# The last transform's second half: whole rows in 4 KB runs read in step 14, and the rows of the last two steps read over them from DRAM buffers of their own

## The chip, the cores and the metric

The kernel runs on one core of one Trainium2 chip. The time is the device time of one execution in microseconds (us). The core has the engines PE (matrix products), DVE, ACT and POOL (elementwise work) and SP, which here only issues DMA copies; ACT and POOL issue some copies too. Sixteen DMA engines move the data of the copies.

## The reference

One layer on 2048 rows of 512 channels in float32. Three of its lines matter here:

```python
h = _layernorm(x, axis=-1) * (1 + ca) + sa
x = x + ga * _A_ref(h, ...)        # long convolution, one filter of 2048 taps per channel
x = x + gb * _B_ref(_layernorm(x) * (1 + cb) + sb, ...)   # shift mixing and an MLP
```

`_A_ref` builds the filter K from the state-space parameters, multiplies the spectra of the padded filter and the padded input, transforms back and keeps the first 2048 rows:

```python
Yf = Uf * Kf[None, :, :, :]
y = irfft2(Yf, s=(1, L2))[:, :, 0, :L]
```

The change lies in this transform back.

## The kernel before, in words

First the kernel builds the filter, normalises the input and stores the first part of its transform in DRAM (`VU`); this takes up to about 225 us, and its long loop runs small pieces of other work from lists called `side`, one list per turn. From 345 us on it only mixes (`_B_ref`). Between lie the sixteen steps (225 to 306 us) and the last transform.

A step is a pair (jh, kc): jh is the half of the 512 channels, kc one of eight groups of four frequencies k1. Step n multiplies the spectra of its group (`spectrum_k` at line 680, `multiply` at 690 and 692), and the step after it runs `back` (702) for it: eight matmuls with `Gm`, two ACT evictions into a tile z of 128 partitions by 4 by 256, and two stores of 256 KB each on POOL's queue into the DRAM buffer `ZT[jh]` (706). z holds for each of 64 output columns j, twice (real and imaginary part n), the group's four frequencies.

The last transform (`inv_half`, line 731) needs for its column block k (four columns j; eight blocks per half of the channels) the rows of all 32 frequencies. So `load_inv` (721) reads a block of 512 KB that gathers from the stores of all eight steps of a half: 128 partitions by 4 by 256, into one of seven buffers of the pool `ldp`, which also holds the `VU` loads. An output group g of `inv_half` needs four blocks: groups 0 and 3 need blocks 3, 7, 0, 4, groups 1 and 2 need 1, 5, 2, 6. Each `inv_half` is 32 matmuls, and DVE adds the result to X2.

The order is written by hand. For half 0: blocks 0, 3, 4, 7 are issued in step 10 on SP, group 0 runs in step 12, group 3 in step 13, blocks 1, 2, 5, 6 are issued in step 13, group 1 runs after step 15 and group 2 behind it. For half 1 nothing is read before the last store: `back` of step 15 stores in two halves on SP's and ACT's queues, then come blocks 3, 7, 0, 4 in halves on both queues, blocks 1, 5, 2, 6 on SP, then a few matmuls that fill the time (`keep`), then group 3's half at 313.63 us and so on with mixing between, group 1 first at 325.52 us.

Each engine works in its own program order. A DMA-issuing instruction waits in that order too, so what SP has to wait for holds back all copies behind it. The framework adds the waits: a load waits for the stores that wrote what it reads (all eight steps of the half), and for the last reader of its buffer.

Of the kernel before, what the change touches and what calls it, by code (L numbers as in the profile page):

```python
# [7 lines left out]
F32 = mybir.dt.float32  # L8
# [19 lines left out]
def shape_constants():  # L28
    f = lambda x: np.ascontiguousarray(x.astype(np.float32))
    k1, k2, q = np.arange(32), np.arange(64), np.arange(32)  # L30
    c2b = lambda c: np.where(c < 32, 31 - c, c)
    th = 2 * np.pi * (k1[None] + .5) * q[:, None] / 64
    W = np.stack([np.cos(th), -np.sin(th)], 1)
    Wt = W.transpose(0, 2, 1)
    FU = np.stack([np.stack([Wt, -Wt[..., ::-1]], 1), np.stack([Wt, Wt[..., ::-1]], 1)])
    FU = np.stack([FU, FU])
    FK = np.zeros((2, 2, 32, 2, 64))
    FK[:, 0, :, 0] = FK[:, 1, :, 1] = W.reshape(32, 64)
    b = c2b(np.arange(64))
    al = 2 * np.pi * b[:, None, None] * ((k1[None, :, None] + .5) / 4096 + k2[None, None, :] / 64)  # L40
    c, s = np.cos(al), np.sin(al)
    T2 = np.stack([np.stack([c, -s], 2), np.stack([s, c], 2)]).reshape(128, 32 * 128)
    be = np.arange(32) + .5
    al = 2 * np.pi * be[:, None, None] * ((k1[None, :, None] + .5) / 4096 + k2[None, None, :] / 64)
    TU = np.stack([np.cos(al), np.sin(al), np.cos(al), -np.sin(al)]).reshape(128, 32 * 64)
    al = 2 * np.pi * be[None, :] * k2[:, None] / 64
    cs = np.stack([np.cos(al), np.sin(al)], 2).reshape(64, 64)
    Gm = np.tile(np.concatenate([cs, cs], 1), (2, 1))
    sg = np.array([1.0, -1.0])[:, None]
    th = 2 * np.pi * (k1[:, None, None, None] + .5) * (sg * be[:, None, None] + 64 * q) / 4096  # L50
    FI = np.stack([np.cos(th), -sg * np.sin(th), -np.sin(th), -sg * np.cos(th)]) * (2 / 4096)
    eye = np.eye(16)
    j = np.arange(32)
    c0 = np.tile((eye[:, :, None] * (j + .5)).reshape(16, 512), (2, 1))
    C0 = np.zeros((2, 2, 32, 2, 512))
    C0[:, 0, :, 0], C0[:, 1, :, 1] = c0, c0
    C0 = C0.reshape(128, 1024)
    e1 = (eye[:, :, None] * j).reshape(16, 512)
    e2 = (eye[:, :, None] * np.ones(32)).reshape(16, 512)
    C1 = np.concatenate([e1, e1, e2, e2] * 2, 0)  # L60
    ex0 = np.concatenate([np.arange(31, -1, -1), np.arange(32, 64)])
    ex1 = np.concatenate([64 * np.arange(8), 512 * np.arange(4)])
    CE = np.concatenate([(eye[:, :, None] * ex0.reshape(2, 32)[:, None, None, :]).transpose(1, 0, 2, 3).reshape(16, -1),
                         np.zeros((16, 64 * NX1))], 1)
    CE = np.tile(CE, (8, 1))
    for u in range(4):
        CE[u * 32:u * 32 + 32, 1024 + u * 16 * NX1:1024 + (u + 1) * 16 * NX1] = \
            np.tile((eye[:, :, None] * ex1).reshape(16, -1), (2, 1))
    PA = np.zeros((2, 4, 16, 2, 2, 4, 2, 16))
    PB = np.zeros((4, 2, 16, 4, 4, 2, 4, 16))  # L70
    for e in range(16):
        for v in range(2):
            for u in range(4):
                for p in range(2):
                    PA[v, u, e, v, p, u, p, e] = 1
        for c in range(8):
            for p in range(4):
                PB[c // 2, c % 2, e, c // 4 * 2 + c % 2, p, 1 - c // 2 % 2, p, e] = 1
    return {k: f(v) for k, v in dict(
        FU=FU.reshape(128, 128), FK=FK.reshape(128, 128), T2=T2, TU=TU, G=Gm,  # L80
        FI=FI.reshape(128, 32 * 64), C0=C0, C1=C1, CE=CE, PA=PA.reshape(128, 512), PB=PB.reshape(128, 2048), ID=np.eye(128)).items()}

# [20 lines left out]
def dram(t, off, ap):  # L103
    return bass.AP(tensor=t.tensor, offset=t.offset + off, ap=ap)


def body(ctx, tc, A):
    nc = tc.nc
    V, S, P, T, Y = nc.vector, nc.scalar, nc.gpsimd, nc.tensor, nc.sync
    pool = lambda name, bufs=1, **k: tc.tile_pool(name=name, bufs=bufs, **k)  # L110
    glob = ctx.enter_context(pool("glob"))
    dpool = ctx.enter_context(pool("dscr", space=DRAM))
# [3 lines left out]

    VU = dpool.tile([2, 64, 64, 256], F32, name="VU")
    ZT = [dpool.tile([128, 32, 256], F32, name=f"ZT{i}") for i in range(2)]
    GD = dpool.tile([4, 128, 20, 128], F32, name="GD")
    WD = {k: dpool.tile(list(A[k].shape), F32, name="D" + k) for k in ("w2", "w3", "w4")}  # L120

# [52 lines left out]
    up = a12.enter_context(pool("up", bufs=2))  # L174
# [15 lines left out]
    C0 = ph.tile([128, 1024], F32R, name="C0")  # L190
# [315 lines left out]
    side = {k: [] for k in range(40)}  # L506
    for k in range(8):
        w, i = ("w3", k) if k < 4 else ("w4", k - 4)
# [26 lines left out]
    def load_tu():  # L535
        TU.append(wml.tile([128, 32, 64], F32, name="wm"))
        Y.dma_start(TU[0], A["TU"].rearrange("p (a b) -> p a b", a=32))

    side[24].append(load_t2)
    side[29].append(load_tu)  # L540
    side[31].append(load_t2)
# [153 lines left out]
    def back(jh, kc):  # L695
        zc = zcs.pop((jh, kc))
        z = s2.tile([128, 4, 256], F32, name="z")
        o = [psa.tile([128, 2, 256], F32, name="pz") for kk in range(2)]
        for n in range(2):
            for kk in range(2):  # L700
                r = slice(kk * 64, kk * 64 + 64)
                T.matmul(o[kk][n * 64:n * 64 + 64], Gm[r, n], zc[n][r], start=True, stop=True, skip_group_check=True)

        def store(q, a, b):
            for n in range(2):
                q.dma_start(dram(ZT[jh], n * 16384 + (kc * 4 + a) * 256, [[32768, 32], [8192, 2], [1, (b - a) * 256]]),
                            z[n * 64:n * 64 + 64, a:b].rearrange("p k d -> p (k d)"))

        last = (jh, kc) == (1, 7)
        for kk in range(2):  # L710
            act(z[:, 2 * kk:2 * kk + 2], o[kk])
            if last:
                store((Y, S)[kk], 2 * kk, 2 * kk + 2)
        if not last:
            store(P, 0, 4)

    def load_inv(jh, k, i=None, q=Y):
        if (jh, k) not in zis:
            zis[jh, k] = block()
        a, n = (0, 4) if i is None else (2 * i, 2)  # L720
        q.dma_start(zis[jh, k][:, a:a + n], dram(ZT[jh], (k * 4 + a) * 32768, [[256, 128], [32768, n], [1, 256]]))

    def load_x(g):
        Y.dma_start(X2[:, g * 4:g * 4 + 4].rearrange("p b d -> p (b d)"), A["x"][g])
# [372 lines left out]
    with tc.manual_schedule():  # L1097
# [11 lines left out]
        for n, st in enumerate(steps):  # L1109
            p = spectrum_k(*st)  # L1110
            multiply(*st, us, p)
            if n == 7:
                v0x.close()
                pw2 = ctx.enter_context(pool("pw2", side="right", reuse_waits="tile"))
                pw1 = ctx.enter_context(pool("pw1", side="right", reuse_waits="tile"))
                W2h, W2l, ldw2 = weights(pw2, WD["w2"], 512, 512, "w2", 4)
                W1h, W1l, ldw1 = weights(pw1, A["w1"], 512, 512, "w1", 4)
            if n > 0:
                back(*steps[n - 1])
            if n == 15:  # L1120
                i1 = inverse_parts(0, 1, psb, "pk2")
            if n < 15:
                us = spectrum_u(*steps[n + 1])
            if n + 3 < 16:
                load_vu(*steps[n + 3])
            if n % 2 == 0 and n < 14:
                flip(steps[n + 2][1])
            if n in (3, 4, 6, 8):
                load_x(n - 3 if n < 5 else n // 2 - 1)
            if n == 9:  # L1130
                Y.dma_start(FI, A["FI"].rearrange("p (a b c) -> p a b c", a=32, b=2))
            if split:
                split()
                split = None
            if n in (8, 9):
                split = ldw1(two, n % 2 * 2, 2)
            if n == 10:
                for k in (0, 3, 4, 7):
                    load_inv(0, k)
            if n == 12:  # L1140
                inverse(0, 0)
                w2s = [ldw2(None, 2 * i, 2) for i in range(2)]
                for b in range(4):
                    half_stat(b, 0)
            if n == 13:
                inverse(0, 3)
                for k in (1, 2, 5, 6):
                    load_inv(0, k)
            if n in (14, 15):
                w2s.pop()()  # L1150
        for f in i1:
            f()
        back(*steps[15])
# [10 lines left out]
            for _ in range(n):  # L1164
                T.matmul(d, W1h[:, 0, :128], W1h[:, 0], start=True, stop=True)

        for k, i in ((3, 1), (0, 0)):
            load_inv(1, k, i, Y)
            load_inv(1, k + 4, i, S)
        for k, i in ((3, 0), (0, 1)):  # L1170
            load_inv(1, k, i)
            load_inv(1, k + 4, i)
        for i in range(2):
            inv_half(0, 2, i, psy, "py")()
        for b in (14, 15, 4, 5, 6, 7):
            half_stat(b, 0)
        for k in (1, 2):
            load_inv(1, k)
            load_inv(1, k + 4)
        keep(6)  # L1180
        inv_half(1, 3, 1, psy, "py")()
        first_stats(7)
# [119 lines left out]
```

## Time and profile before

| | |
|---|---|
| median of three runs | 689.6 us (687.0, 689.6, 690.3) |
| profiled execution | 691.26 us, its span 689.5 us, mean granted clock 0.989 |
| PE busy | 642.6 us, 93% of the span |
| DVE, ACT, POOL busy | 498.0, 331.2, 124.8 us |
| DMA | 86.42 MB, 125 GB/s over the span |
| chain that ended last | PE 70%, DVE 6%, DMA 5%, ACT 3% |

The profile gives, for each stretch of time, each engine's busy time with the number of instructions, the clock granted to PE, the share of time in which the 16 DMA engines were busy, and GB/s. A row of the timeline has start, duration, engine, line, operation, output and inputs; in brackets stands how long the engine had been idle before, and what it waited for. SPq and ACTq are the queues in which SP and ACT issue copies; the duration there is that of issuing. In the DMA views a packet is one run of contiguous bytes.

### The profile page before, as it was taken

To read this page: it belongs to the slowest core of one execution; us is meant where nothing else is said; L and a number is where in the kernel's file an instruction comes from. 1 tells how busy PE (TensorE), PEld (TensorE's weight loads), DVE (VectorE), ACT (ScalarE), POOL (GpSimd) and SP (SyncE) were. 2 spreads that over 40 slices of the span, in tenths; PEclk is the share of its full clock that TensorE was granted. 3 is DMA by queue.
4 is the path that set the end of the run, shared out by engine and by line. 5 is a ranking of instruction groups with operands and counts; after the bars stand their busy time and mean duration, and the time that the engine had idled before them with its cause. 6 is when DMAs were issued, how large, how long until landed. Compare 5 with 4: busy or idle time off the path is not lost.

```text
span 689.5 us, 16884 instructions
## 1 busy us (share of the span) xinstructions
PE 642.6 (93%) x7195; PEld 509.2 (74%) x7195; DVE 498.0 (72%) x795; ACT 331.2 (48%) x505; POOL 124.8 (18%) x236
## 2 busy tenths in 40 slices
PE   1899999999999998977998999999999999999996
PEld 0456655655569776634887889999899889898895
DVE  7899999999996887986987967464574536363522
ACT  3878988889875557432444623123131312222121
POOL 4011112112103355413741101001010000000000
PEclk9999999999999999998999999999999999999999
DMA  8603264643739997967387010020100201010001
GB/s 299 284 2 79 75 218 105 209 121 85 275 85 317 354 335 258 346 204 226 108 257 240 1 32 32 16 77 15 47 31 17 77 1 62 1 49 13 1 31 31
DMA packets 51091, 86.42 MB, mean 125 GB/s; under 512 B 4676, under 2 KB 39496, under 8 KB 48424
## 3 DMA queue, kind: packets, MB, share of 16 engines
q1 hardware_dynamic: 46712, 66.74, 30.1%
q0 software_dynamic: 3440, 17.57, 7.4%
q8 instruction: 56, 0.92, 0.6%
q10 hardware_dynamic: 864, 1.05, 0.5%
q14 instruction: 19, 0.16, 0.1%
HBM read 59.12 MB, written 32.90 MB: 133 GB/s over the span
## 4 chain that ended last, share of the span: by engine, by line
PE 70%; DVE 6%; DMA 5%; ACT 3%; POOL 2%; issue 1%; ACTq 0%; SPq 0%; DVEq 0%; POOLq 0%
PE pm L841 7%; PE pm L838 7%; PE pm L839 7%; PE xx L448 7%; PE pa L954 6%; PE pa L955 6%; PE pa L962 6%; PE kp L498 3%; DMA ZT<-z 3%; PE ph L893 2%; PE ph L895 2%; PE ph L892 2%; DMA ld<-ZT 2%; PE pu L426 2%; PE pT L803 2%; PE pk L626 2%
## 5 line engine op out<-in xcount | busy, mean ns | idle before, releaser
L115 ACT ACTIVATE gh<-pm 128x512 fp32r<-128x512 f32 (+1 forms) x48 | 26.9, 560 | 200.7 <-PE pm L841 200.7
L838 PE MATMUL pm<-nh,w3h 128*128 128x256 f32 (+1 forms) x352 | 86.6, 281 | 2.7 <-ACT nh L115 2.7
L839 PE MATMUL pm<-nh,w3l 128*128 128x256 f32 (+1 forms) x352 | 86.3, 280 | 0.1
L946 DVE TENSOR_TENSOR gl<-gf,gh 128x512 fp32r<-128x512 f32 (+1 forms) x48 | 30.8, 643 | 68.4 <-ACT gf L115 68.4
L954 PE MATMUL pa<-w4h,gh 128*128 128x512 f32 (+1 forms) x176 | 69.6, 395 | 0.0
L838 PEld LDWEIGHTS pm<-nh,w3h 128*128 128x128 f32 (+1 forms) x352 | 66.0, 187 | 4.4 <-ACT nh L115 2.9
L955 PE MATMUL pa<-w4l,gh 128*128 128x512 f32 (+1 forms) x176 | 68.9, 392 | 0.0
L839 PEld LDWEIGHTS pm<-nh,w3l 128*128 128x128 f32 (+1 forms) x352 | 65.9, 187 | 2.2 <-DVE w3l L756 0.5
L765 POOL TENSOR_TENSOR rs<-mv,eps_t 128x1 f32<-128x1 f32 (+1 forms) x39 | 11.0, 282 | 282.4 <-DVE mv L771 265.4
L841 PE MATMUL pm<-nl,w3h 128*128 128x256 f32 (+1 forms) x352 | 55.0, 278 | 0.0
L449 PE MATMUL xx<-MG,ON 64*128 64x512 f32 x160 | 48.1, 397 | 0.0
L962 PE MATMUL pa<-w4h,gl 128*128 128x512 f32 (+1 forms) x176 | 48.0, 390 | 0.0
L448 PE MATMUL xx<-MG,ON 64*128 64x512 f32 x160 | 48.0, 396 | 0.0
L841 PEld LDWEIGHTS pm<-nl,w3h 128*128 128x128 f32 (+1 forms) x352 | 47.0, 187 | 0.0
L898 DVE TENSOR_TENSOR h<-h,ph 128x512 f32<-128x512 f32 x16 | 11.0, 687 | 45.1 <-PE ph L895 45.1
L466 DVE SCALAR_TENSOR_TENSOR e<-tr,p 128x512 f32<-128x512 f32 x64 | 41.1, 684 | 1.5 <-ACT tr L115 1.5
L498 PEld LDWEIGHTS kp<-e,e 128*32 128x32 f32 x2048 | 30.1, 110 | 12.7 <-issue 7.6
L475 DVE TENSOR_TENSOR e<-tr,p 128x1024 f32<-128x1024 f32 x32 | 39.0, 1220 | 0.0
L476 DVE TENSOR_TENSOR e<-tr,m 128x1024 f32<-128x1024 f32 x32 | 39.0, 1219 | 0.0
L115 ACT ACTIVATE p<-xx 128x1024 f32<-128x1024 f32 (+1 forms) x40 | 37.5, 979 | 2.2 <-PE xx L252 1.0
L962 PEld LDWEIGHTS pa<-w4h,gl 128*128 128x128 f32 (+1 forms) x176 | 33.0, 188 | 7.3 <-DVE gl L946 0.2
L115 ACT ACTIVATE tr<-xx 128x1024 f32<-128x1024 f32 x32 | 33.0, 1030 | 9.6 <-PE xx L449 7.9
(236 smaller groups left out, 1731.6 us busy)
## 6 DMA issues: line engine op xcount, KB each, us to landing
VU<-vs SPq DMA_DIRECT2D x64, 128.0 KB, 3.7
ld<-VU SPq DMA_DIRECT2D x16, 512.0 KB, 7.4
ZT<-z POOLq DMA_DIRECT2D x30, 256.0 KB, 6.2
ld<-ZT SPq DMA_DIRECT2D x12, 512.0 KB
Dw<-in_w POOLq DMA_DIRECT2D x8, 688.0 KB, 4.7
xu<-in_u SPq DMA_DIRECT2D x4, 1024.0 KB, 8.0
KX<-in_x SPq DMA_DIRECT2D x4, 1024.0 KB, 8.0
GD<-go SPq DMA_DIRECT2D x16, 256.0 KB, 2.3
```

The lines of the kernel that those rows point to most:

```text
L115: return S.activation(out, in_, f, bias=bias, scale=scale)
L448: T.matmul(x[:, :512], la, ma, start=(i == 0), stop=(i == len(ops) - 1))
L449: T.matmul(x[:, 512:], lb, mb, start=(i == 0), stop=(i == len(ops) - 1))
L466: V.scalar_tensor_tensor(e0[:, 1, a], tr[:, 1, 0], 1.0 - 2.0 * a, mg[:, a], op0=OP.mult, op1=OP.mult)
L475: V.tensor_mul(e0[:, 0], tr[:, 0, 0:1].to_broadcast([128, 2, 512]), mg)
L498: T.matmul(kp[32 * j:32 * j + 32, (k % 2) * 4 + g], e1[:, r, d], e0[:, r, :, d * 32:d * 32 + 32], start=(r == 0), stop=(r == 1), skip_grou ...
L838: T.matmul(p, wh[:, k, c], hi[k], start=(k == 0), stop=False)
L839: T.matmul(p, wl[:, k, c], hi[k], start=False, stop=False)
L841: T.matmul(p, wh[:, k, c], lo[k], start=False, stop=(k == 3))
L954: T.matmul(acc[i], gh[:m, e, s], W4h[:m, f], start=(f == 0), stop=False)
L955: T.matmul(acc[i], gh[:m, e, s], W4l[:m, f], start=False, stop=False)
L962: T.matmul(acc[i], gl[:m, e, s], W4h[:m, f], start=False, stop=(f == 10))
```

## The change

The layout of `ZT` changes so that the four columns of a block lie together: a run of a block is now 4 KB where it was 1 KB, and a store's run is 1 KB where it was 4 KB. The constants `FI` and `Gm` are permuted to match. A block's partitions are now ordered by half of the columns, part, frequency within the group, and step; so the rows of steps 14 and 15 are every seventh and eighth partition.

The stores of steps 14 and 15 go to two DRAM buffers of their own, `ZL[0]` and `ZL[1]`. Blocks 3, 7, 0, 4 of half 1 are read whole from `ZT[1]` in step 14, when only six of its eight steps are stored; 3 and 7 go into a tile `zx` in the pool `up`, 0 and 4 into the pool `ldp`. Afterwards `load_late` writes the 16 partitions of step 14 (issued on POOL in step 15) and the 16 of step 15 (on SP and ACT, behind the last store) over them, 64 KB each. Blocks 1, 5, 2, 6 are issued behind the last store as before, each followed by its two late copies on SP. Two stores in the loop that builds the filter's spectrum write the constant `C0` into the places of `ZT[1]` that no step writes any more, 512 KB each.

```diff
-    cs = np.stack([np.cos(al), np.sin(al)], 2).reshape(64, 64)
+    cs = np.stack([np.cos(al), np.sin(al)], 1).reshape(64, 64)
...
+    FI = FI.reshape(2, 2, 8, 4, -1).transpose(1, 0, 3, 2, 4)
...
+    ZL = [dpool.tile([8, 2, 32, 256], F32, name=f"ZL{i}") for i in range(2)]
...
+    for i in (6, 7):
+        side[i + 8].append(lambda i=i: Y.dma_start(dram(ZT[1], i * 16384, [[131072, 8], [1024, 16], [1, 1024]]), C0.bitcast(F32)))
...
+        last = (jh, kc) == (1, 7)
+        zt, o0, sa = (ZL[kc - 6], 0, 16384) if jh and kc > 5 else (ZT[jh], kc * 16384, 131072)
+
         def store(q, a, b):
             for n in range(2):
-                q.dma_start(dram(ZT[jh], n * 16384 + (kc * 4 + a) * 256, [[32768, 32], [8192, 2], [1, (b - a) * 256]]),
-                            z[n * 64:n * 64 + 64, a:b].rearrange("p k d -> p (k d)"))
-
-        last = (jh, kc) == (1, 7)
+                q.dma_start(dram(zt, o0 + (n * 4 + a) * sa, [[256, 64], [sa, b - a], [1, 256]]),
+                            z[n * 64:n * 64 + 64, a:b])
...
-    def load_inv(jh, k, i=None, q=Y):
-        if (jh, k) not in zis:
-            zis[jh, k] = block()
-        a, n = (0, 4) if i is None else (2 * i, 2)
-        q.dma_start(zis[jh, k][:, a:a + n], dram(ZT[jh], (k * 4 + a) * 32768, [[256, 128], [32768, n], [1, 256]]))
+    def load_inv(jh, k, t=None):
+        t = zis[jh, k] = block() if t is None else t
+        Y.dma_start(t.rearrange("p b d -> p (b d)"), dram(ZT[jh], k * 1024, [[8192, 2], [16384, 64], [1, 1024]]))
+
+    def load_late(k, i, q):
+        q.dma_start(zis[1, k].rearrange("(m x) b d -> m x (b d)", x=8)[:, 6 + i],
+                    dram(ZL[i], k * 1024, [[8192, 2], [16384, 8], [1, 1024]]))
...
+            if n == 14:
+                zx = up.tile([128, 2, 4, 256], F32, name="xu")
+                for i, k in enumerate((3, 7)):
+                    load_inv(1, k, zx[:, i])
+                for k in (0, 4):
+                    load_inv(1, k)
+            if n == 15:
+                for k in (3, 7, 0, 4):
+                    load_late(k, 0, P)
...
-        for k, i in ((3, 1), (0, 0)):
-            load_inv(1, k, i, Y)
-            load_inv(1, k + 4, i, S)
-        for k, i in ((3, 0), (0, 1)):
-            load_inv(1, k, i)
-            load_inv(1, k + 4, i)
+        for k in (3, 0):
+            load_late(k, 1, Y)
+            load_late(k + 4, 1, S)
...
-        for k in (1, 2):
+        for k in (1, 5, 2, 6):
             load_inv(1, k)
-            load_inv(1, k + 4)
+            for i in range(2):
+                load_late(k, i, Y)
```

In the patterns a pair is [step in elements, count], the outermost first.

SP's order around steps 10 to 13, before (`ld<-ZT_61` is a block of half 0, `ld<-VU` the input's spectrum, `w2l` a weight; the words in brackets are the semaphores waited for: DMASW of copies issued by POOL, DMAHW of copies issued by SP or ACT, else of an engine):

```order
L721 DMA ld<-ZT_61 128x4x256 [waits DMAHW3_49,PE_49]
L721 DMA ld<-ZT_61 128x4x256 [waits DMAHW5_49,DMAHW4_49,DVE_49]
L721 DMA ld<-ZT_61 128x4x256 [waits PE_49]
L640 DMA ld<-VU 128x4x256 [waits DMAHW6_49,DMAHW0_49,DVE_49]
L640 DMA ld<-VU 128x4x256 [waits DMAHW7_49,PE_49]
```

and in the changed kernel:

```order
L725 DMA ld<-ZT_61 128x1x1024 [waits DMAHW5_49,PE_49]
L725 DMA ld<-ZT_61 128x1x1024 [waits DMAHW7_49,DMAHW6_49,DVE_49]
L725 DMA ld<-ZT_61 128x1x1024 [waits PE_49]
L644 DMA ld<-VU 128x4x256 [waits DMAHW2_49,DMAHW0_49,DVE_49]
L644 DMA ld<-VU 128x4x256 [waits DMAHW1_49,PE_49]
```

The order is the same; a block is one row of 1024 per partition now.

SP's order at the end of the steps, before (`ZT_62` is `ZT[1]`):

```order
L706 DMA ZT_62<-z 32x2x512 [waits Activation_49,Pool_49]
L706 DMA ZT_62<-z 32x2x512 [waits DMAHW0_49]
L721 DMA ld<-ZT_62 128x2x256 [waits DMASW6_49,DMASW7_49,DMASW5_49,DMAHW0_49,DMASW4_49,DMAHW1_49,DMASW3_49,DMAHW2_49,DMASW2_49,DMAHW6_49,DMASW1_49,DMAHW7_49,DMASW0_49,PE_49]
L721 DMA ld<-ZT_62 128x2x256 [waits DMAHW4_49,PE_49]
L721 DMA ld<-ZT_62 128x2x256 x3
L721 DMA ld<-ZT_62 128x2x256 [waits PE_49]
L721 DMA ld<-ZT_62 128x4x256 [waits DMAHW2_49,PE_49]
```

and in the changed kernel (`ZL_63` and `ZL_64` are `ZL[0]` and `ZL[1]`):

```order
L725 DMA xu<-ZT_62 128x1x1024 [waits DMASW4_49,DMASW3_49,DMASW5_49,DMASW2_49,DMASW6_49,DMASW1_49,DMASW7_49,DMASW0_49,Pool_49]
L725 DMA xu<-ZT_62 128x1x1024 [waits DMAHW1_49]
L725 DMA ld<-ZT_62 128x1x1024 [waits DMAHW2_49,PE_49]
L725 DMA ld<-ZT_62 128x1x1024 [waits DMAHW3_49,PE_49]
L713 DMA ZL_64<-z 64x2x256 [waits DMAHW5_49,Activation_49]
L713 DMA ZL_64<-z 64x2x256 [waits DMAHW7_49]
L728 DMA xu<-ZL_64 16x1x1024 [waits DMAHW5_49,DMAHW6_49,DMAHW4_49,DMAHW7_49,DMAHW1_49,DMAHW0_49]
L728 DMA ld<-ZL_64 16x1x1024 [waits DMAHW3_49,DMAHW2_49]
L725 DMA ld<-ZT_62 128x1x1024 [waits PE_49]
L728 DMA ld<-ZL_63 16x1x1024 [waits DMAHW4_49,DMASW4_49,DMASW3_49]
L728 DMA ld<-ZL_64 16x1x1024
L725 DMA ld<-ZT_62 128x1x1024 [waits PE_49]
```

Four blocks now stand ahead of the last store's half on SP; behind it a block, two late copies that wait for that block's landing (DMAHW), the next block, and so on four times. The order on PE and DVE is the same in both kernels.

## The prediction

> **What bounds the kernel now.** I read the page's engine totals first, then the windows from 225 us on, the waits there, the chain, and last the DMA view of single stretches. PE is busy for 642.6 of 689.5 us, so the end is set by PE's program order; the change can move it only by what PE waits for. The stretch that the change touches is short:
>
> ```profile
> 225.00:255.00 30.00, 28.15 (x635) 22.25 (x626) 24.23 (x40) 16.79 (x34) 11.70 (x14) 1.00 0.98 349
> 255.00:285.00 30.00, 26.24 (x545) 19.77 (x542) 26.30 (x44) 18.63 (x38) 16.72 (x20) 1.00 0.88 292
> 285.00:300.00 15.00, 13.52 (x304) 8.71 (x297) 14.27 (x26) 8.52 (x18) 6.06 (x8) 1.00 0.92 323
> 306.00:314.00 8.00, 1.55 (x7) 0.78 (x6) 2.38 (x7) 0.00 (x0) 0.00 (x0) 0.90 0.75 234
> 314.00:326.00 12.00, 11.36 (x97) 6.99 (x99) 9.59 (x21) 2.44 (x4) 5.89 (x16) 0.78 0.70 224
> 345.00:690.00 345.00, 335.06 (x2160) 302.51 (x2160) 190.86 (x320) 95.20 (x175) 28.60 (x74) 0.99 0.16 51
> ```
>
> First PE's busy time, last three numbers its granted clock, the DMA share and GB/s. In the sixteen steps (225 to 306) the DMA engines are nearly full; from 306 to 314 PE stands still for want of data; after 345 PE is 97% busy and nothing there can absorb a delay. PE's own rows give the dates that the new loads must meet:
>
> ```profile
> 283.77 1.93 PE L731 MATMUL pz<-ld,FI 128*32 128x256 f32 x32
> 289.26 1.93 PE L731 MATMUL pz<-ld,FI 128*32 128x256 f32 x32
> 299.59 1.93 PE L731 MATMUL pk<-ld,FI 128*32 128x256 f32 x32 [1.48 <-DMA ld<-ZT]
> 313.63 4.09 PE L731 MATMUL py<-ld,FI 128*32 128x256 f32 x32 [6.45 <-DMA ld<-ZT]
> 325.52 1.93 PE L731 MATMUL py<-ld,FI 128*32 128x256 f32 x32
> ```
>
> These are the last transform's groups: (0,0) and (0,3) on the first four loads of ZT[0]; (0,1) on the second four; at 313.63 the first of ZT[1], on rows 3, 7, 0, 4; at 325.52 the first on rows 1, 5, 2, 6. SP issues their loads at
>
> ```profile
> 269.70 4.17 SPq L721 DMA_DIRECT2D ld<-ZT  x4
> 278.27 0.91 SPq L640 DMA_DIRECT2D ld<-VU  x2
> 279.24 1.02 SPq L750 DMA_DIRECT2D w2l<-Dw  x2
> 283.90 8.53 SPq L721 DMA_DIRECT2D ld<-ZT  x4
> 303.93 1.18 SPq L706 DMA_DIRECT2D ZT<-z  x2
> ```
>
> and the chain between 304 and 314 is store, load, PE:
>
> ```profile
> 305.03 2.69 DMA ZT<-z
> 308.51 4.98 DMA ld<-ZT
> 313.63 2.42 PE py L731 x17
> ```
>
> **The change, part by part.** *Constants.* FI and Gm are permuted; the matmuls keep count and shape: nothing.
>
> *The loads' pattern.* Before, a 512 KB load walks DRAM as 128 times 4 runs of 1 KB; now as **2** times 64 runs of 4 KB. What may that outermost 2 do? The DMA view shows how many engines a copy uses, because each engine that took part leaves one packet of a few bytes:
>
> ```profile
> DMA packets 256, 0.26 MB, mean 114 GB/s; under 512 B 15, under 2 KB 255, under 8 KB 255
> DMA packets 160, 0.52 MB, mean 142 GB/s; under 512 B 32, under 2 KB 32, under 8 KB 160
> DMA packets 90, 0.66 MB, mean 438 GB/s; under 512 B 4, under 2 KB 6, under 8 KB 14
> ```
>
> The first row (331.0 to 333.3) holds one GD copy, outermost count 128: 15 small packets, with one record missing, so 16 engines. The second (300.5 to 304.2) holds one step's two stores, outermost 32: 32 small packets, 16 each. The third (13.5 to 15.0) holds the four DS copies of line 325, whose outermost count is 1: 4 small packets, one each. Every other copy of this kernel has outermost counts that 16 divides. So in all the trace a copy is dealt over its outermost dimension: 16 engines, or one. It doesn't prove the rule for 2, since a DS copy has only one run to deal. By the likeliest reading the new loads run on 2 of 16 engines, 64 runs each, and always the same two.
>
> [...]
>
> *What a load then costs.* One engine's price of bytes, from two full stretches (22 to 27 us, 8 KB runs; 309 to 325, 1 KB runs) and the landing of a 256 KB copy on 16 engines:
>
> ```profile
> q1 hardware_dynamic: 292, 2.12, 100.8%
> q1 hardware_dynamic: 3744, 3.67, 71.5%
> GD<-go SPq DMA_DIRECT2D x16, 256.0 KB, 2.3
> ```
>
> 1.008×16×5 us/2.12 MB makes 10.0 us per 256 KB (counted as 0.262 MB) on one engine in 8 KB runs; 0.715×16×16/3.67 makes 13.1 in 1 KB runs. Runs of 4 KB lie between; with one fixed share per run and one per byte I get 10.4. The bounds are 10.0 and 13.1. A 512 KB load has 256 KB per engine: **10.4 us**, and the next waits behind it. The fixed part is 2.3−13.1/16 = 1.5 us. On 16 engines a load would take 1.3 us plus that.
>
> *First four loads.* Issued at 269.7: 4×10.4 = 41.6, plus 1.5, plus what four steps' stores take of the same two engines (two stores per step, 10.0 to 13.1 over 16 each, 1.5 us a step: 6). They land at 319. PE's 283.77 becomes 319: **+35**. Cover: none, PE is in order and 14 us is all the lead there is.
>
> *Second four.* Ahead in the queue are the two VU and two w2l loads, 1.5 each, to 325. Then 41.6 and 4.5 for three steps' stores: 371. PE's 299.59 becomes 371: **+71** in all. The steps 13 to 15 themselves run inside this wait.
>
> *Rows 3, 7, 0, 4 of ZT[1], whole, in step 14.* Four more loads on the same pair: 412.6. Their wait for the stores of the first six steps of the half costs nothing here, those are done by 330. SP's half of the last store stands behind these loads in SP's own queue, lands by 413.5, and then the late rows: SP waits for the load and the store, issues two copies of 16 runs; each is on the pair for 8×0.16 = 1.3 us plus 1.5 fixed. PE's 313.63 becomes 419: **+105**. The early read is thus no read ahead of the last store at all.
>
> *Rows 1, 5, 2, 6.* Each load is followed by two late copies that wait for its landing, and SP is in order, so the next load is issued only after them. A round: 0.4 issue, 1.5 fixed, 10.4, 0.8 for two issues, and about 1.6 in which the late rows hold the pair: 14.7. Four rounds from 415 end at 474, the last late copy lands at 476. PE's 325.52 becomes 476: **+150**. What PE has to do between (the mixing of two blocks, 12 us) lies inside that wait.
>
> *The rest.* The two fill stores go out in the loop that builds the kernel's spectrum, inside this window:
>
> ```profile
> 60.00:210.00 150.00, 146.14 (x2598) 91.51 (x2598) 144.35 (x187) 127.88 (x155) 24.23 (x36) 0.99 0.50 146
> ```
>
> Half of the DMA time is free there: nothing (bound: 512 KB on 8 engines, 2×5 us, if nothing covered it). The stores write 1 KB runs instead of 4 KB: 0.8 instead of 0.65 us on each engine, two a step; sixteen steps at 2×0.15 us make 5 us at most while the engines are full, inside the waits. POOL issues four late copies more, about 0.55 us each, at the end of its steps, before nothing that is due. The clock falls after a stand (0.90 and 0.78 in the rows above), which I price at 0 to 5 us for the four long waits, and take 0 to 1.
>
> Sum: 689.5 + 150 = 839.5, say **840 us**. The profiled run was 691.26 and the median 689.6, so the span stands for the median.
>
> **The rivals.** *Two engines, but not always the same* (each load on another pair). For: the trace shows no pair. Then four loads go abreast, land in 12 to 15 us, and the first two groups meet their dates nearly (269.7+1.5+10.4+2 = 284 against 283.77; 283.9+14 = 298 against 299.59). The early read, free at 302 (next rival), lands at 315, and what is left are the four serial rounds, 14.7 each from 316 on, plus 2 for the last late copy: 377 against 325.52, **+51, 741 us**.
>
> *All 16 engines, and the rounds in the way.* The early loads wait for the store of step 13 (issued 295.44, landing 6.2 by the stores' median), so go at 302; 2 MB beside the last stores take 6 to 8 us. The last store lands at 307.7 (305.03+2.69), its late copies at 311 to 312: PE starts at 312 to 313 instead of 313.63. The stores' issue rows behind these dates, and their landing:
>
> ```profile
> 295.44 1.07 POOL L706 DMA_DIRECT2D ZT<-z  x2 [4.35 <-ACT z L115]
> 299.61 1.07 POOL L706 DMA_DIRECT2D ZT<-z  x2 [3.10 <-ACT z L115]
> ZT<-z POOLq DMA_DIRECT2D x30, 256.0 KB, 6.2
> ```
>
> But the four rounds, now 4.2 us each (0.4+1.5+1.3+0.8 and some landing), end at 328.5 to 330.5 instead of before 325.5: +3 to +5, **693 us**.
>
> *The other side: the early read pays.* Also with 16 engines: PE's 6.45 us stand at 313.63 shrinks by up to 3 us (311 is the earliest at which the last rows are in), and with it the slow clock of 314 to 326, 12×0.22 = 2.6 us. It decides if a round takes under 3.2 us, so that the four are done by 325: 689.5−5.7 = **684 us**. Against it: both parts need a full deal over 16 engines.
>
> **How the numbers follow.** Same two engines 0.80; changing pairs 0.05; sixteen engines with the rounds in the way 0.10, of which 0.06 beyond half a per cent and 0.04 within; the early read pays 0.05. The first has most because every copy of the trace is dealt by its outermost count, and the new one's is 2; the last two share what the missing proof leaves. Half a per cent, 3.4 us, is what a measurement of this kernel can tell from no change (its three runs spread over 3.3). So: faster 0.05, same 0.04 and 0.01 for gain and loss cancelling, slower 0.90. The likeliest case's own range: sixteen loads at 10.0 to 13.1 are −6 to +43, and the rounds' landings ±8: 815 to 880. It holds nine tenths of that case, 0.72; reached down over the changing pairs it adds their 0.05 and the case's lower tail: 730 to 880, about 0.81.
>
> **What would show it.** Right: the loads of the last transform land tens of us after issue, with 2 small packets each; stretches between 290 and 470 at a DMA share near 0.13 and about 50 GB/s; PE waits for them of about 35, 36, 34 and 45 us at the lines of the last transform; the other stages as long as before. Wrong: loads that land in 3 to 8 us with 16 small packets; then the 693 or the 684 holds, told apart by whether PE waits before the group that stood at 325.52. A load of 6 us at 10 GB/s per engine on more engines would mean that neither reading of the deal is right.

## The result, and the profile after

The changed kernel takes 849.08 us (median of four runs, 847.83 to 853.12) against 689.43 before: a ratio of 1.233, 95% interval 1.228 to 1.239. Its profiled run took 847.83, its span 846.1 us.

The windows of the changed kernel (as before: PE's busy time first, last the granted clock, the DMA share and GB/s), one for each long wait and one for the rest:

```profile
283.00:318.00 35.00, 0.00 (x0) 0.00 (x0) 0.00 (x0) 0.00 (x0) 2.93 (x2) 0.55 0.37 108
332.00:368.00 36.00, 3.48 (x80) 2.28 (x72) 8.45 (x14) 5.21 (x11) 2.52 (x4) 0.58 0.25 78
376.00:412.00 36.00, 0.38 (x2) 0.00 (x0) 1.59 (x5) 0.00 (x0) 1.73 (x3) 0.54 0.20 65
432.00:475.00 43.00, 0.87 (x6) 0.64 (x6) 7.61 (x16) 2.63 (x4) 3.54 (x12) 0.55 0.11 44
...
480.00:845.00 365.00, 355.20 (x2344) 320.69 (x2344) 202.14 (x341) 102.67 (x187) 38.44 (x101) 0.99 0.16 54
```

In four stretches, 150 us together, PE does 4.7 us of work, and the DMA engines, at a share of 0.88 to 0.98 from 225 to 300 us before the change, are at 0.11 to 0.37. Behind them the kernel runs as it did. PE's timeline at the last transform:

```profile
318.71 3.64 PE L739 MATMUL pz<-ld,FI 128*32 128x256 f32 x32 [37.67 <-DMA ld<-ZT]
326.71 1.93 PE L739 MATMUL pz<-ld,FI 128*32 128x256 f32 x32
368.28 3.63 PE L739 MATMUL pk<-ld,FI 128*32 128x256 f32 x32 [32.80 <-DMA ld<-ZT]
421.35 0.73 PE L739 MATMUL py<-ld,FI 128*32 128x256 f32 x2 [44.98 <-DMA ld<-ZL]
481.66 3.36 PE L739 MATMUL py<-ld,FI 128*32 128x256 f32 x32 [48.47 <-DMA ld<-ZL]
```

These groups stood at 283.77, 289.26, 299.59, 313.63 and 325.52. From the last of them to the end it is 846.1−481.66 = 364.4 us, and was 689.5−325.52 = 364.0: all of the loss lies in these four waits. What a load looks like (DMA view from 350 to 360 us):

```profile
DMA packets 128, 0.52 MB, mean 52 GB/s; under 512 B 2, under 2 KB 2, under 8 KB 128
q1 hardware_dynamic: 128, 0.52, 12.8%
```

In 10 us about one load's packets pass (126 of 4 KB and 2 small ones), at 12.8% of 16 engines, which is 2 engines. Over two engines that is 2×10/126, some 160 ns for a packet, and the 64 packets that a load has on each engine take 10.2 us. SP's issues show the queue filling up:

```profile
267.45 1.30 SPq L725 DMA_DIRECT2D ld<-ZT  x2
...
281.12 11.06 SPq L725 DMA_DIRECT2D ld<-ZT  x1
...
292.28 9.88 SPq L644 DMA_DIRECT2D ld<-VU  x1
```

The first two issues take 1.30 us together, the fourth 11.06 and the `VU` load behind it 9.88, about as long as a load. And the chain of waits behind the last store, with the four serial rounds (store, then load and late copies four times):

```profile
391.26 20.93 DMA ZL<-z
412.27 0.53 SPq L728
...
413.46 17.02 DMA ld<-ZT
...
431.62 14.08 DMA ld<-ZT
...
446.86 14.43 DMA ld<-ZT
...
462.41 14.10 DMA ld<-ZT
...
477.05 4.47 DMA ld<-ZL
481.66 3.36 PE py L739 x32
```

A store of 128 KB that took 2.69 us before takes 21 behind the early loads.

### The profile page after: what moved, and what is told of

The parts are those of the page before. It is cut to its first block, busy times and chain, and to the rows that moved or that the text cites. A ratio compares the mean times of both kernels' runs of the same rounds, so it can differ in the third digit from the quotient of the medians.

```text
span 846.1 us, 16921 instructions
## 1 busy us (share of the span) xinstructions
PE 646.5 (76%) x7195; PEld 514.9 (61%) x7195; DVE 497.9 (59%) x795; ACT 331.4 (39%) x505; POOL 129.1 (15%) x240
## 4 chain that ended last, share of the span: by engine, by line
PE 57%; DMA 22%; DVE 3%; SPq 3%; POOL 2%; ACT 2%; issue 1%; ACTq 0%; DVEq 0%; POOLq 0%
DMA ld<-ZT 16%; PE xx L450 6%; PE pm L849 6%; PE pm L847 6%; PE pm L846 5%; PE pa L962 5%; PE pa L963 5%; PE pa L970 5%; PE kp L500 3%; DMA ZL<-z 2%; PE pu L428 2%; PE pk L630 2%; PE ph L901 2%; PE ph L903 2%; PE ph L900 2%; SPq L725 1%
## 5 line engine op out<-in xcount | busy, mean ns | idle before, releaser
L739 PE MATMUL py<-ld,FI 128*32 128x256 f32 x112 | 11.4, 472 | 93.4 <-DMA ld<-ZL 93.4
L739 PEld LDWEIGHTS py<-ld,FI 128*32 128x32 f32 x112 | 6.8, 133 | 96.1 <-issue 95.2
L742 DVE TENSOR_TENSOR KX<-py,KX 128x512 f32<-128x512 f32 x8 | 5.4, 678 | 91.6 <-PE py L739 91.6
L116 ACT ACTIVATE z<-pz 128x512 f32<-128x512 f32 x32 | 17.4, 596 | 102.8 <-PE pz L706 86.8
L116 ACT ACTIVATE go<-pm 128x512 f32<-128x512 f32 x16 | 9.5, 596 | 83.7 <-PE pm L849 76.6
L116 ACT ACTIVATE h<-h,nm,rs 128x512 f32<-128x512 f32 x16 | 12.8, 812 | 67.9 <-POOL nm L836 67.7
```

The costliest lines, as they stand in the source:

```text
L116: return S.activation(out, in_, f, bias=bias, scale=scale)
```

## The experiments

Theory: the loads run on two engines because the outermost count of their pattern is 2. Rivals: the new layout is slow by itself (stores in 1 KB runs, loads in 4 KB runs), or the new waits and order on SP are.

### Each load as two copies of 64 partitions

```diff
-        Y.dma_start(t..., dram(ZT[jh], k * 1024, [[8192, 2], [16384, 64], [1, 1024]]))
+        for s in range(2):
+            Y.dma_start(t[s * 64:s * 64 + 64], dram(ZT[jh], k * 1024 + s * 8192, [[16384, 64], [1, 1024]]))
```

The late copies are cut in the same way into two of 8 partitions.

> The changed kernel with each 512 KB load issued as two copies of 64 partitions (outermost count 64 instead of 2) and each late copy as two of 8 partitions; layout, runs of 4 KB, order, waits and constants as in the change. Theory (two engines because of the outermost 2): loads land in 3 to 5 us, the waits of about 35 us at the groups of the last transform vanish, and what is left are the four serial rounds on SP, now with twice the issues: 0.8+1.5+1.3+1.6 and some landing, 5 to 6 us a round, so the group on rows 1, 5, 2, 6 starts near 333 to 335: 696 to 700 us. Rival (the new layout, with 1 KB runs in the stores or 4 KB runs in the loads, is slow by itself): still above 800 us. Rival (waits and issue order on SP): still above 800 us, since no order and no wait changes but for more issues.

Measured: 712.35 us, ratio 1.033 (1.029 to 1.038). The same bytes in the same places with the same waits, and 137 of the 160 us are gone; both rivals are out as the cause of the bulk. The remainder is larger than I forecast (696 to 700): the four rounds took 6.5 to 7.5 us each by SP's issues, where I had 5 to 6, and the first group is late behind the last store. PE's timeline:

```profile
300.00 2.26 PE L742 MATMUL pk<-ld,FI 128*32 128x256 f32 x32 [1.94 <-DMA ld<-ZT]
320.76 1.03 PE L742 MATMUL py<-ld,FI 128*32 128x256 f32 x3 [13.57 <-DMA ld<-ZL]
345.57 3.76 PE L742 MATMUL py<-ld,FI 128*32 128x256 f32 x32 [12.54 <-DMA ld<-ZL]
```

The first half's groups are on time again; the second half's start 7 and 20 us late.

### The outermost count 128, 4 and 8

The dense order: a block's partitions ordered by step, part, frequency, half of the columns.

```diff
-    FI = FI.reshape(2, 2, 8, 4, -1).transpose(1, 0, 3, 2, 4)
+    FI = FI.reshape(2, 2, 8, 4, -1).transpose(2, 0, 3, 1, 4)
...
-        ... dram(ZT[jh], k * 1024, [[8192, 2], [16384, 64], [1, 1024]])
+        ... dram(ZT[jh], k * 1024, [[8192, 128], [1, 1024]])
```

> The change with the partitions of a block ordered by step, part, frequency and half of the columns, so that a load is 128 equal steps of 4 KB (outermost count 128) and a late copy 16 (outermost count 16, contiguous partitions); FI permuted to match; same number of copies, same order and waits as the change. Theory: 16 engines, rounds of 0.5+1.5+1.3+1.0 and some landing, 4.2 to 4.6 us each, the group on rows 1, 5, 2, 6 at 328 to 331 instead of 325.5: 692 to 695 us. Rival (early read pays): rounds under 3.2 us, 684 us. Rival (layout or waits): above 800 us.

The late copies become 16 equal steps onto 16 contiguous partitions; this holds for the next two runs too, so that only the loads' count differs between the three.

With a gap of 4 KB in the buffer the same load can't be told as 128 equal steps. The gap behind every second step of the kernel:

```diff
-        ... [[8192, 128], [1, 1024]]
+        ... [[263168, 4], [8192, 32], [1, 1024]]
```

> As the dense order, but a gap of 4 KB in the DRAM buffer behind every second step makes the load's pattern 4 times 32 runs of 4 KB instead of 128. Nothing else changes. Theory (engines follow the outermost count): 4 engines, 5.2 us a load; the first group near 294, the second pair near 325, the first of the second half near 350, rounds of 9 us, the group on rows 1, 5, 2, 6 near 385: 745 to 755 us, DMA share 0.25 in the waits. Rival (a count that 16 does not divide falls to one or two engines whatever it is): above 840. Rival (only the count 2 or the strides matter): as the dense order, 692 to 695.

The gap behind every step:

```diff
-        ... [[8192, 128], [1, 1024]]
+        ... [[132096, 8], [8192, 16], [1, 1024]]
```

> As the dense order, with a gap of 4 KB behind every step: the load's pattern is 8 times 16 runs of 4 KB. Theory: 8 engines, 2.6 us a load; the groups of the first half meet their dates, rounds of 6.2 us, the group on rows 1, 5, 2, 6 near 340: 701 to 707 us. Rival (any count not divisible by 16 is slow): above 800. Rival (strides do not matter): 692 to 695.

Measured: 702.85 us with 128 (ratio 1.019, 1.015 to 1.023); in one run each, 732.85 with 8 and 762.3 with 4; the changed kernel with 2: 849.08. The order of the four follows the count, and a gap of 4 KB alone costs 30 or 59 us, so neither "any such count falls to one or two engines" nor "the count does not matter" holds. SP's queue (q1) with nothing but loads of the count 4 (323 to 328 us; most packets outside the second row are POOL's):

```profile
DMA packets 141, 0.53 MB, mean 107 GB/s; under 512 B 12, under 2 KB 12, under 8 KB 140
q1 hardware_dynamic: 113, 0.45, 21.9%
```

The loads alone, 0.45 MB in 5 us, are 90 GB/s on 21.9% of 16 engines, which is 3.5 engines; with the count 2 it was 52 GB/s on 12.8%. With the count 8 SP's queue stands at 50.6% from 336 to 340 us, which is 8.1 engines. A load leaves 2 small packets with the count 2, 4 with 4 (113 packets, of which 109 have 4 KB) and 8 with 8 (344 to 349 us, below). So in these runs the engines follow the outermost count: 2.0, 3.5 and 8.1.

All three came out slower than forecast, against the upper ends by 8 us (128), 26 (8) and 7 (4). With the count 8 I had the first half's groups on time; they were not:

```profile
291.96 3.23 PE L739 MATMUL pz<-ld,FI 128*32 128x256 f32 x32 [9.60 <-DMA ld<-ZT]
316.16 3.64 PE L739 MATMUL pk<-ld,FI 128*32 128x256 f32 x32 [8.64 <-DMA ld<-ZT]
337.52 0.73 PE L739 MATMUL py<-ld,FI 128*32 128x256 f32 x2 [12.22 <-DMA ld<-ZL]
366.24 3.74 PE L739 MATMUL py<-ld,FI 128*32 128x256 f32 x32 [16.84 <-DMA ld<-ZL]
```

My sum left out that these engines were already busy: at the share of 0.88 that the window of 255 to 285 had before, an engine has 26.4 of 30 us of work, and four loads on 8 engines instead of 16 add, by my estimate of 10.4 us for 256 KB on one engine, 5.2 to each of the eight, more than the 3.6 that are free. That gives the sign; that it explains all 8 us is argued, not shown. The trace holds a second part that my sum lacked, the price of a packet. One of the later loads with the count 8, alone in the queue (344 to 349 us):

```profile
DMA packets 129, 0.50 MB, mean 99 GB/s; under 512 B 8, under 2 KB 8, under 8 KB 129
q1 hardware_dynamic: 129, 0.50, 30.1%
```

That is 0.301×16×5 us for 121 packets of 4 KB, 200 ns each; in another such stretch (336 to 341 us) it is 287. The count 4 has 0.219×16×5/109 = 160, as the count 2 has. So the four rounds took 7.0 to 8.6 us instead of my 6.2. Why a packet costs more with 8 was not taken apart.

What is left with 16 engines shows in SP's issues and PE's two waits of the dense order:

```profile
314.23 0.42 SPq L725 DMA_DIRECT2D ld<-ZT  x1
318.55 0.78 SPq L728 DMA_DIRECT2D ld<-ZL  x2
319.38 0.41 SPq L725 DMA_DIRECT2D ld<-ZT  x1
...
332.90 0.77 SPq L728 DMA_DIRECT2D ld<-ZL  x2
```

```profile
317.77 0.73 PE L739 MATMUL py<-ld,FI 128*32 128x256 f32 x2 [10.89 <-DMA ld<-ZL]
335.52 3.93 PE L739 MATMUL py<-ld,FI 128*32 128x256 f32 x32 [5.92 <-DVE st L792]
```

Four rounds of 4.5 to 5.2 us (4.2 in my forecast) put the group on rows 1, 5, 2, 6 at 335.52, and the first group starts at 317.77 instead of 313.63. For the later one the profile names DVE as what ended the wait; the last late copy, issued at about 333.3 and 2.1 us on its way by these copies' median, is in at the same moment. The next runs take the two delays apart.

### The loads first, then the late copies

```diff
         for k in (1, 5, 2, 6):
             load_inv(1, k)
+        for k in (1, 5, 2, 6):
             for i in range(2):
                 load_late(k, i, Y)
```

> The dense order (16 engines) with the four loads of rows 1, 5, 2, 6 issued one after another and the eight late copies behind them, instead of four rounds of load, wait, two late copies. Theory (the dense order's remaining loss of 12 us has two parts: the last store lands 5 us later because 2 MB of early loads are ahead of it, so the first group starts at 317.8 instead of 313.6; and the four serial rounds of 4.6 to 5 us put the group on rows 1, 5, 2, 6 at 335.5): this edit takes the second part away. Loads landed near 321, late copies near 326; the group comes at its place behind the first, 325.5+4.1: 329 to 331, total 693 to 696 us against 702.9. Rival (the whole loss is the slow clock after the late store): 701 to 703. Rival (everything comes from the store): as before the edit.

Measured: 692.26 us, ratio 1.006 (1.004 to 1.009), just under the forecast. The group on rows 1, 5, 2, 6 starts at 327.98 instead of 335.52 and waits for nothing. So some 10 us of the dense order's 14 (702.85 against 688.9 for the kernel before beside it) were the serial rounds. The chain shows the other part, the last store:

```profile
303.54 8.39 DMA ZL<-z
...
312.50 3.48 DMA ld<-ZL
```

### The dense layout alone

No early read, no late copies, no buffers of their own, no fill stores; blocks 3 and 0 whole on SP and 7 and 4 on ACT behind the last store.

```diff
-        for k in (3, 0):
-            load_late(k, 1, Y)
-            load_late(k + 4, 1, S)
+        for k in (3, 0):
+            load_inv(1, k, q=Y)
+            load_inv(1, k + 4, q=S)
```

> The dense layout alone: loads of 4 KB runs over 16 engines, stores of 1 KB runs, but no early read, no late copies, no DRAM buffers for the last two steps and no fill stores; all eight blocks of the second half are read whole behind the last store, rows 3 and 0 on SP, 7 and 4 on ACT. Theory (the early read delays the last store): with it gone the store lands near 307.5 as before; 2 MB instead of the first 1 MB ahead of the first group cost 1 to 2 us, the loads' cheaper runs take some back: first group at 314 to 315.5, 690 to 692 us. Rival (the stores' 1 KB runs cost the 5 us): first group at 317 or later, 694 or more. Rival (4 KB runs are a gain of their own): 684 to 688.

Measured: 692.08 us, ratio 1.004 (1.003 to 1.006). The chain:

```profile
304.94 2.83 DMA ZT<-z
...
308.51 6.93 DMA ld<-ZT
```

The store, in the same 1 KB runs, lands in 2.83 us: its 8.4 came from the bytes ahead of it. The load ahead of the first group takes 6.93 instead of 4.98, as it is 2 MB instead of 1.

### No overlap between early and late rows: 96 and 32 partitions, 80 and 48

```diff
-        ... t ..., dram(ZT[jh], k * 1024, [[8192, 128], [1, 1024]])
+        e = 96 if jh else 128
+        ... t[:e] ..., dram(ZT[jh], k * 1024, [[8192, e], [1, 1024]])
```

and one late copy of the remaining 32 partitions, which waits for the last stores only.

> Dense layout; a block of the second half is read as its first 96 partitions (steps 8 to 13) and its last 32 (steps 14 and 15, one DRAM buffer of their own), which do not overlap, so nothing waits for a load's landing before the late copy; rows 3, 7, 0, 4 early in step 14 as in the change. No fill stores. Theory: the serial rounds vanish; 1.5 MB instead of 2 MB stand ahead of the last store, which lands near 311, the late rows near 314.5: 690 to 693 us. Rival (early reads ahead of the store cost nothing): first group at 311 to 312, 685 to 688.

With 80 and 48, the read of blocks 3 and 7 in step 13:

```diff
-        e = 96 if jh else 128
+        e = 80 if jh else 128
...
-            if n == 14:
+            if n == 13:
                 zx = ...
```

> As the run with 96 early partitions, but 80 early (steps 8 to 12) and 48 late, and the early read of rows 3 and 7 issued in step 13, so that it waits for the store of step 12 and can go near 296 instead of 301.5. Theory (what counts is that the early bytes are through before the last store at 304): most of 1.25 MB is through by 303, the store lands near 308, the late rows (0.75 MB) near 312, the first group 1 to 2 us before its old date: 685 to 689 us. Rival (the DMA engines are full until 300 and the early read pushes the loads of the first half's second group, due at 299.6): that group 2 to 3 us late, 690 to 693.

Measured: 692.81 us (ratio 1.005, 1.004 to 1.007) and 693.17 (1.006, 1.004 to 1.007). The second missed its forecast of 685 to 689. Its chain, with the store quicker than 8.4 us (in at 309.4, forecast near 308) and the late rows in at 316.5 instead of near 312:

```profile
304.73 4.62 DMA ZL<-z
...
309.93 6.57 DMA ld<-ZL
```

The late rows met a price that I had not known. Both of the following rows are DMA views with the queue full and only loads of 4 KB runs on it; the first is of the 96 and 32 partitions (315 to 321 us):

```profile
DMA packets 470, 1.53 MB, mean 255 GB/s; under 512 B 96, under 2 KB 96, under 8 KB 470
q1 hardware_dynamic: 470, 1.53, 104.3%
```

the second of the dense layout alone, 128 partitions (314 to 318 us):

```profile
DMA packets 469, 1.66 MB, mean 416 GB/s; under 512 B 63, under 2 KB 63, under 8 KB 469
q1 hardware_dynamic: 443, 1.62, 100.3%
```

Copies of 96 and 32 partitions move 255 GB/s where those of 128 move 416: 1.043×16×6 us for 374 packets of 4 KB is 268 ns each, and the other view has 163 (66.1 us of both queues for 406). With 80 and 48 it is 239 GB/s (316 to 323 us). This fits the slow late rows; no run separates it from the rest.

### Halves, and an early read of only what the first group needs

The dense layout alone with blocks 3, 7, 0, 4 in halves of 2 KB runs, as the kernel before orders them:

```diff
-            load_inv(1, k, q=Y)
-            load_inv(1, k + 4, q=S)
+        for k, i in ((3, 1), (0, 0)):
+            load_inv(1, k, i, Y)
+            load_inv(1, k + 4, i, S)
+        for k, i in ((3, 0), (0, 1)):
+            load_inv(1, k, i)
+            load_inv(1, k + 4, i)
```

> The dense layout alone, but rows 3, 7, 0, 4 of the second half read in halves (runs of 2 KB, 1 MB first) behind the last store, in the order of the kernel before. Theory (the layout-alone run lost 2 us because 2 MB instead of 1 MB stand ahead of the first group): first group at 313 to 314 as before, total 687.5 to 690 us, no difference from before. Rival (4 KB and 2 KB runs are a gain): 685 to 687. Rival (the 1 KB runs of the stores cost): 691 to 693.

Measured: 690.19 us, ratio 1.000 (0.999 to 1.002): the layout by itself is worth nothing, either way. Its longer runs are cheaper for an engine (10.2 us for 256 KB in 4 KB runs, measured above, against 13.1 in 1 KB runs in the prediction's working), but no time came of it. To it, 96 partitions of the four halves that the first group needs, in step 14, and 32 behind the store:

```diff
+            if n == 14:
+                ...
+                for k, i in ((3, 1), (7, 1), (0, 0), (4, 0)):
+                    load_inv(1, k, i, p=slice(0, 96))
...
-            load_inv(1, k, i, Y)
-            load_inv(1, k + 4, i, S)
+            load_inv(1, k, i, Y, slice(96, 128))
+            load_inv(1, k + 4, i, S, slice(96, 128))
```

> As the dense halves, but of the halves that the first group needs, the 96 partitions of steps 8 to 13 are read in step 14 (0.75 MB, ahead of the last store) and the 32 of steps 14 and 15 behind it (0.25 MB); the other halves and rows 1, 5, 2, 6 are read whole behind the last store. One DRAM buffer, no fill stores, no wait between early and late copies. Theory (what hurts is the bytes ahead of the last store; 0.75 MB fit into the gap of 301 to 305): store lands at 308 to 309, late rows at 311.5 to 312.5, first group 1 to 2 us before its old date: 686 to 689 us. Rival (any early bytes delay the store by as much as they save): 689 to 692.

Measured: 688.83 us, ratio 0.998 (0.996 to 1.000). This is the best version of the study, one microsecond faster than the kernel before; that is less than I called measurable, and I don't claim it as a gain. The total lies in the forecast, but its mechanism does not show in the profiled runs: the first group on rows 3, 7, 0, 4 starts at 312.22, and at 311.81 without the early read; the one on rows 1, 5, 2, 6 at 323.76, and at 323.85 without.

### The same two engines?

The changed kernel with the first half's eight loads issued by POOL:

```diff
-        Y.dma_start(t..., dram(ZT[jh], k * 1024, [[8192, 2], [16384, 64], [1, 1024]]))
+        q.dma_start(...)      # q = P for jh = 0
```

> The changed kernel (loads of 2 times 64 runs on two engines), with the eight loads of the first half issued by POOL instead of SP; the second half's stay on SP. Leaves nothing out. Theory (same two engines for every such copy, whatever issues it): first group again near 319, second near 370, total 840 to 860 us. Rival (copies issued by POOL take changing pairs of engines): four loads go abreast, the groups of the first half meet their dates within a few us, and only the second half is late: four early loads 302 to 344, then four rounds of 15.2 us, the group on rows 1, 5, 2, 6 near 410: 770 to 780 us.

Measured: 815.76 us in one run, between the two forecasts. The DMA view of the four loads (294 to 299 us; q0 is POOL's queue):

```profile
q0 software_dynamic: 232, 0.92, 46.5%
q1 hardware_dynamic: 67, 0.13, 6.8%
```

46.5% of 16 engines is 7.4, as many as four loads of two engines each take when they go abreast; SP's loads stay at 12.8%, 2 engines, with several of them issued. So the loads that SP issues share two engines here, and the four that POOL issues do not. Which engines these were, no view here shows. The time fell between because POOL gave out the loads late, at 279.17 instead of 267.45, and the second four at 313.32; the first group started at 303.19, and the second half, whose loads stayed on SP, had waits of 49 and 48 us, where the changed kernel has 45 and 48.

### The early read behind the last store

The loads-first kernel with the read of blocks 3, 7, 0, 4 moved from step 14 to behind the last store:

```diff
-            if n == 14:
-                ...
         back(*steps[15])
+        ... load_inv(1, k) for 3, 7, 0, 4, then load_late(k, 0, P)
```

> The dense order with the loads first, but the whole read of rows 3, 7, 0, 4 (and POOL's late copies of step 14) put behind the last store in program order instead of in step 14; nothing else moves. Theory (the early bytes hold up the last store): the store lands 2.7 to 3.2 us after its issue instead of 8.4, near 307.5; the loads, now behind it, are in near 312, their late copies near 314 to 315, so the first group at 314 to 316 against 316.2: 690 to 692.5 us; the early read is worth nothing. Rival (the store is slow because of its own 1 KB runs or its buffer): store still 8 us, first group near 322, 697 to 700. Rival (the early read does gain): first group at 318 or later with a quick store, 694 to 697.

Measured: 698.81 us (ratio 1.015, 1.012 to 1.017), against a forecast of 690 to 692.5. The store's part held: in the stretch from 306.2 to 309 only the loads' 4 KB packets are left,

```profile
DMA packets 244, 0.93 MB, mean 331 GB/s; under 512 B 18, under 2 KB 18, under 8 KB 244
```

that is, the store, issued from 302.2 on, was through by 306.2. But my "worth nothing" fell. The chain:

```profile
305.82 8.09 DMA ld<-ZT
...
314.45 5.71 DMA ld<-ZL
```

Load and late copy now come one after the other behind the store, and the first group starts at 320.25 instead of 316.23. With late copies in the kernel the early read is worth about 6 us (698.81 against 692.26, and 5.9 by the two ratios); it only buys back what the late copies cost, since without both (692.08, and 690.19 in halves) the time is no worse.

## Why the prediction was right

The time lay in the range, 849 against 840, and the mechanism was the forecast one, step by step:

| step | forecast | measured |
|---|---|---|
| a load on its two engines | 10.4 us | 10.2 |
| first group of half 0 | 319 | 318.71 |
| second | 371 | 368.28 |
| first group on rows 3, 7, 0, 4 | 419 | 421.35 |
| first group on rows 1, 5, 2, 6 | 476 | 481.66 |
| span | 839.5 | 846.1 |

That the first dates agree within 3 us is in part luck. SP issued its first load at 267.45, 2.3 us before the forecast's 269.7. Counted from there, and then from group to group, the four stretches took 51.3, 49.6, 53.1 and 60.3 us, and the forecast has 49.3, 52, 48 and 57. The terms put at nothing held as far as the trace tells: the first loads went out no later than before the change, so the fill stores ahead of them cost nothing that shows.

**The deal.** "The new loads run on 2 of 16 engines" was the whole of it, and it rested on a thin row: four copies with one small packet each. The two small packets and the 12.8% show it, the runs with 128, 8, 4 and 64+64 that the outermost count is the cause. One row was misread beside it: in the first view not one record is missing but 17 (255 where 256 runs and 16 small packets make 272), as many as one engine's whole share; 16 engines stays the likeliest reading. The chance of 0.80 was fair for that evidence; the row of the count 1 could not exclude the other reading. That it is always the same two engines no row of before shows; it was my estimate, and the runs showed 2 engines (12.8%) for SP's loads issued one behind the other, and 7.4 (46.5%) for four of POOL's. The 8 engines of the fill stores, which only the bound of 2×5 us uses, no row of before shows either: in the changed kernel a fill store leaves 8 small packets (DMA view from 116 to 121 us).

**What was mis-sized** are the two terms with late copies. The four rounds, 14.7 us each, took 18.2, 15.2, 15.6 and 15.1 from start to start (the last to the end of its issues), 5.3 us more in all, and the last late copy 4.5 instead of 2; as they began 1.5 us before the forecast's 415, the last group comes some 6 us late. And from the last store's landing to the first group on rows 3, 7, 0, 4 it was 9.2 us instead of 5.5. Both meet in one place: SP and ACT each issued two late copies between 412 and 414 us, and SP the first round's load right behind. From 414 to 418 us both queues together stand at 12.3% of 16 engines, 6.8 and 5.5, which is 2 engines. My sum had only SP's two on the pair, and those gone when the rounds began. That this is all of the excess is argued. The rest of the gap to the median, about 3 us, is outside the span and between runs: the profiled run took 847.83.

**The range.** Its terms don't add up to its bounds: −6 to +43 and ±8 about 840 make 826 to 891, not 815 to 880. The measured 849 lies in both.

**The queue.** I let every issue cost 0.4 us; with the pair full, a load's issue took 10 to 12. That held back the `VU` loads behind them as well (292.28 instead of 278.27), but PE shows no long wait for those, and the later loads were bound for the same pair anyway.

**The clock.** Taken at 0 to 1 us. It fell to 0.55 in the waits, and the first groups behind them took 3.6 instead of 1.93 us, but most of that lies inside the next wait: from the last group to the end it is 0.5 us.

**The rivals.** The case "16 engines, the rounds in the way" had its mechanism right, and the dense order shows it, but at 702.85 and not 693: it lacked the early loads ahead of the last store, 5 us, and its rounds were 4.5 to 5.2 instead of 4.2. "The early read pays" is not borne out: it gained about 6 us only beside late copies, which cost as much, and nothing that the timeline shows in the best version. More than one pair shows on POOL's queue only: 46.5% of 16 engines, 7.4, with four loads.

## What to carry to other kernels

Look at the outermost count of a copy's DRAM pattern before its run length: an order of dimensions that turns 128 equal steps into 2 times 64 cost 146 us here (849.08 against 702.85), a gap that makes it 4 times 32 cost 59, and the longer runs of the new layout gave nothing (690.19 with them in halves, ratio 1.000). The row to look for is a long wait for a load while the DMA share stands at 2/16, here 12.8%. What is read early is also ahead in the queue: when the engines are full, count what stands behind it, above all the last store of a chain (8.39 us behind the early loads of the dense layout, 2.83 without them). In these kernels a second copy over a part of what the first wrote waits for it: with the dense order SP issues a block's late copies at 318.55, 4.3 us after the load's 314.23. With two parts that don't overlap the wait is gone (311.78 after 311.33 with 96 and 32 partitions), but here the copies of fewer partitions were slower (255 GB/s against 416) and ate what that saved (692.81 us against 692.26).

## What the runs showed of the hardware that I had not expected

- The copies to 96 and 32 partitions are slow per byte though they are dealt over all engines (96 small packets in six copies): 255 GB/s, against 416 with 128, both with 4 KB runs and the engines full. A packet of 4 KB takes 268 ns instead of 163. The same price per packet, 160 ns, holds for loads of 128 partitions on two and on four engines, but on eight engines it was 200 to 287. What makes the difference was not taken apart.
- With loads on two engines, SP's first two issues took 1.30 us together and the next two 22.33 (from 269.85), about as long as two loads at 10.2: my estimate from these rows is that about two of them are outstanding at most.
- The two-engine loads issued by POOL leave far more small packets than those of SP: from 285 to 300 us, with four of them and one step's stores, the DMA view counts

```profile
DMA packets 3157, 3.55 MB, mean 236 GB/s; under 512 B 1960, under 2 KB 2064, under 8 KB 3157
```

  So one small packet for an engine, as the prediction counts them, does not hold for these loads. What the packets are stays open.
